# Attention with two gated layers on one core: run 0's q and k loaded, transposed and split by head pairs, and where the warm matmuls end

## The chip, the cores and the metric

The kernel runs on one core of a Trainium2 chip. The metric is device time in microseconds (us). Shares of the work fall to TensorE (PE, with PEld for its weight loads), VectorE (DVE), ScalarE (ACT), GpSimd (POOL) and the queue of SyncE (SP), from which all DMAs of this kernel are issued.

## What is computed

Windowed attention over 4 batches, 8 heads, 576 positions and head size 64 (each query sees itself and the 127 positions before it, with a bias by distance), then two gated layers over the 2304 tokens. Inputs are float32.

```python
def attention(q, k, v):                      # (4, 8, 576, 64)
    scores = 0.125 * q @ k.transpose(0, 1, 3, 2)
    rel = pos[:, None] - pos[None, :]
    scores = where((rel >= 0) & (rel < 128), scores - slope[h] * abs(rel), -1e9)
    p = exp(scores - scores.max(-1, keepdims=True))
    return (p / (p.sum(-1, keepdims=True) + 1e-9)) @ v

x = attention(q, k, v)                       # as (2304, 512)
x = ((x @ w_a) * (x @ w_b)) @ w_out          # 512 -> 1536 -> 512
out = (((x @ w1) * (x @ w2)) @ w3) @ w_out2  # 512 -> 1024 -> 1024 -> 512
```

## The kernel before

**Split numbers.** Every float32 product is made of three products of a high and a low part (`x_hi`, `x_lo`): ACT copies the high part, DVE subtracts it from the whole (`sub`, line 73). For q and k the parts are `q_th`, `q_tl`, `k_th`, `k_tl` (lines 291 and 292).

**Steps and runs.** A batch has five blocks of queries, four of 128 and one of 64. `RUNS` takes them as blocks (0, 1), (2, 3), (4). A step is one run for one pair of heads; with four pairs, steps 0 to 3 are run 0 of the first batch, steps 4 to 7 its run 1, steps 8 to 11 its run 2, and so on to 59. Step n issues (`attention_ops`, line 675): the scores of the step on PE (`scores`, line 318); on DVE four reductions with the bias, which also give the row's extreme (`step_exps`, line 345), and on ACT four exponentials with their sums (line 351); the product with v of step n - 3 (`pv`, line 404); then some gate work from `Filler`; and for step n - 1 the division on DVE (`norms`, lines 358 to 365: sum plus 1e-9, reciprocal, four multiplications) and the transposes of the quotients on PE (`probs`, line 383), which DVE or ACT copies out as `pt` (line 270 or 268).

**Loads and transposes of q and k.** `load_item` loads one block of q or of k for all 8 heads, 256 KB in pieces of 256 bytes. The first six (four of run 0, two of run 1) go to tiles named `early`, later ones to a ring of five named `raw`. `prep` transposes an item on PE (four transposes, line 282) and splits it. The four items of run 0 are loaded, transposed and split ahead of step 0; those of a later run during the run before it, one a step.

**Weights.** `Stages` (`side`) brings the six weight blocks of the first gate group through `convert`: load (lines 83, 92), two passes on ACT (lines 108, 111), four on DVE (lines 115, 118, 122, 127), the high part on ACT (line 136), the low part on DVE (line 73, tile `wlA`). For each step it makes `PACE` turns. Only two raw blocks are held at a time: a third is loaded when the first has been read.

**Gate work.** `Filler` holds the first group's gate matmuls (`g1`, line 546; `g2_some`, line 574) and gives some to PE in each step, from step 7 on, when the first 256 tokens have passed the attention.

**Warm matmuls.** `keep_warm` (line 373) issues matmuls on a tile of zeros whose result nobody reads: ten of 256 columns at the start, then one of 512 columns after each full block of `pv` of the first batch, two a step for the products of steps 0 to 7.

**What sets the order.** PE's instructions keep the order of the program (`manual_schedule`); those of the other engines are ordered by the scheduler at build time, which fixes each engine's queue. On the chip each engine then takes its queue in that order.

Of the kernel before, what the change touches and what calls it, by code (L numbers as in the profile page):

```python
# [8 lines left out]
F32 = mybir.dt.float32  # L9
# [20 lines left out]

GROUPS = (6, 4)
TA, TN = 256, 512
LEAD, EARLY, RING = 512, 6, 5
CUTS = (0, 1280, 1792, 2304)
RUNS = ((0, 1), (2, 3), (4,))
LAG = 3
# [1 line left out]
FILL = 1.6  # L38
PACE = (2.0, 1.0)
TURN = 400  # L40
WARM_RUNS, WARM = 3, 1


@with_exitstack
def attention_moe_moe(ctx, tc, q, k, v, w_a, w_b, w_o, w_1, w_2, w_3, w_o2, out):
# [193 lines left out]
    def items(run):  # L239
        return [(x, i) for i in blocks_of(run)[1] for x in range(2)] if run < NR else []  # L240
# [10 lines left out]

    def load_item(run, n):
        b, (x, i) = blocks_of(run)[0], items(run)[n]
        if len(items(0)) * run + n < EARLY:
            t = early_p.tile([P, H * D], F32, name="early")
        else:
            t = ring_p.tile([P, H * D], F32, name="raw")
        raws[b, x, i] = t
        load(t, x, b, i)

    def load_v(run, n):
        b, i = blocks_of(run)[0], blocks_of(run)[1][n]
# [9 lines left out]
    def prep(run, n):  # L272
        b, (x, i) = blocks_of(run)[0], items(run)[n]
        m = rows(i)
        hold = []

        def trans():
            ps = ps_t.tile([P, W], F32, name="tr")[:, 0:NP * m].rearrange("p (h c) -> p h c", h=NP)
            hold.append(ps)
            t = raws.pop((b, x, i))  # L280
            for hp in range(NP):
                nc.tensor.transpose(ps[:, hp, :], t[0:m, hp * P:(hp + 1) * P], ident[0:m, 0:m])  # L282

        def parted():
            ps = hold[0]
            if x == 0 and m == LAST:
                dst = [(slice(j * D, (j + 1) * D), q_t2, slice(j * D, (j + 1) * D)) for j in range(2)]
            else:
                dst = [(slice(0, P), k_t if x else q_t, slice(i * P, i * P + m))]
            for o, (hi, lo), c in dst:  # L290
                nc.scalar.activation(hi[o, :, c], ps[o], ACTF.Copy)
                sub(nc.vector, lo[o, :, c], ps[o], f32(hi[o, :, c]))

        return trans, parted

# [88 lines left out]
        t = d["pt"] = sm_p.tile([P, W], F32, name="pt", bufs=PTS)[:, 0:nj * n]  # L384
        evict(nc.scalar if i else nc.vector, t, ps)

    ready = [0]
    outs = {}

    def pv(step):  # L390
# [5 lines left out]
        for i in RUNS[rn]:  # L396
# [9 lines left out]
                        start=(g == 0), stop=(g == nb - 1),  # L406
                    )
            at += m
            if b == 0 and rn < WARM_RUNS and m == P:
                keep_warm(WARM, warm)  # L410

    def pv_out(step):
        b, rn, hp = step
# [261 lines left out]
    def attention_ops():  # L675

        late = []
        for n in range(NS + LAG):
# [5 lines left out]
            if n >= LAG:  # L684
                ops.append(lambda s=steps[n - LAG]: pv(s))
                late_1.append(lambda s=steps[n - LAG]: pv_out(s))
            if hp < len(items(run + 1)):
                f, h = prep(run + 1, hp)
                ops.append(f)
                late_1.append(h)  # L690
# [12 lines left out]
    class Filler:  # L703
# [5 lines left out]
        def run(self, owed):  # L709
            self.owed += owed  # L710
            while self.owed > 0 and self.items:
                f, cost, need = self.items[0]
                if whole.get(0, 0) < 6 or need > min(ready[0], CUTS[len(acc)]):
                    break
                self.items.pop(0)
                self.owed -= cost
                f()
            self.owed = min(self.owed, 1.0)

# [6 lines left out]
    pools["A", 1] = ctx.enter_context(tc.tile_pool(name="wA1", bufs=1))  # L726
    first = ExitStack()
    pools.update(conv=first.enter_context(tc.tile_pool(name="conv_a", bufs=1)), raws=2, cas=3)
    early_p = first.enter_context(tc.tile_pool(name="early_p", bufs=EARLY))
    pools["gate"] = gate_pa  # L730
    pools.update(abufs=1, gbufs=2)

    consts()
    for x in range(len(items(0))):
        load_item(0, x)
    for x in range(len(RUNS[0])):
        load_v(0, x)
    for x in range(len(items(1))):
        load_item(1, x)
        f, g = prep(0, x)  # L740
        f()
        g()
    side.parts += weight_parts(0)
    fl = Filler()
    nc.vector.memset(warm, 0.0)
# [66 lines left out]
```

## Time and profile before

| | |
|---|---|
| time, median of 3 runs | 963.18 us (962.84 to 963.54) |
| profiled execution | 965.76 us, span 964.0 us |
| PE busy | 944.0 us, 98% of the span |
| DVE busy | 552.1 us, 57% |
| ACT busy | 420.6 us, 44% |
| POOL busy | 156.9 us, 16% |
| share of PE in the chain that ended last | 91% |

Busy time is a mean over stages. The profiled execution is one execution: its rows give durations and waits, and its own time lies 2.58 us over the median. "Idle before" in a row is the time in which the engine had nothing to run, with the releaser that ended it. A row's duration reaches to the result; the next instruction of the engine may start somewhat before that.

### The profile page before, as it was taken

What the parts mean: (1) busy time and instruction counts of PE and PEld (TensorE: products, weight loads), DVE (VectorE), ACT (ScalarE), POOL (GpSimd) and SP (SyncE); (2) the same over time, 40 slices, a digit from 0 to 9 for tenths busy, and PEclk for the clock granted to TensorE, in tenths of its full rate; (3) what the DMA queues carried; (4) which work ended last, traced back from release to release, by engine and by line L of the source; (5) the groups of instructions that cost most, each with busy time, mean ns of one, the idle gap of its engine ahead of it and who ended that gap; (6) DMA issues with size and microseconds to landing.
All of it is one profiled execution on the core that took longest, in us unless ns stands there. A gap on an engine that the chain in (4) does not pass through costs nothing.

```text
span 964.0 us, 13974 instructions
## 1 busy us (share of the span) xinstructions
PE 944.0 (98%) x5330; PEld 787.4 (82%) x5330; DVE 552.1 (57%) x1312; ACT 420.6 (44%) x939; POOL 156.9 (16%) x139
## 2 busy tenths in 40 slices
PE   7899999999999999999999999999999999999998
PEld 5588788787888888888888888888888888888886
DVE  6968786854998355866745653822832822521322
ACT  5867777855654344444533531533421421211111
POOL 3000010001112110211110121344212111111111
PEclk8799999999999999999999999999999999999999
DMA  9523333002443222332312320300300300000112
GB/s 213 154 57 71 83 77 68 18 2 88 132 137 103 77 88 91 106 99 78 130 46 97 109 88 1 111 21 0 110 22 1 109 22 1 23 1 0 44 56 99
DMA packets 90371, 68.28 MB, mean 71 GB/s; under 512 B 58304, under 2 KB 79296, under 8 KB 90304
## 3 DMA queue, kind: packets, MB, share of 16 engines
q1 hardware_dynamic: 90304, 67.38, 24.1%
q8 instruction: 42, 0.69, 0.3%
q14 instruction: 25, 0.20, 0.1%
HBM read 58.20 MB, written 8.91 MB: 70 GB/s over the span
## 4 chain that ended last, share of the span: by engine, by line
PE 91%; DVE 5%; ACT 2%; DMA 1%; issue 0%; SPq 0%; POOL 0%; DVEq 0%
PE mm L546 51%; PE mm L598 13%; PE mm L613 10%; PE mm L454 5%; PE tr L404 3%; PE s L318 2%; PE tr L383 2%; PE mm L574 2%; PE tr L282 1%; DVE pe L345 1%; DVE pe L365 1%; ACT pe L351 1%; PE mm L446 1%; PE mm L586 1%; DMA early<-in_k 1%
## 5 line engine op out<-in xcount | busy, mean ns | idle before, releaser
L73 POOL TENSOR_TENSOR gl<-g,gh 128x512 fp32r<-128x512 f32 (+1 forms) x102 | 124.4, 1219 | 790.3 <-ACT gh L558 790.3
L555 DVE TENSOR_TENSOR g<-a,mm 128x512 f32<-128x512 f32 (+1 forms) x102 | 63.4, 622 | 203.1 <-PE mm L546 198.3
L558 ACT ACTIVATE gh<-g 128x512 fp32r<-128x512 f32 (+1 forms) x102 | 59.1, 579 | 152.9 <-DVE g L555 152.4
L553 ACT ACTIVATE a<-mm 128x512 f32<-128x512 f32 (+1 forms) x102 | 55.2, 541 | 126.2 <-PE mm L546 126.2
L546 PE MATMUL mm<-x_hi,wlA 128*128 128x512 f32 (+1 forms) x416 | 102.9, 368 | 0.0
L546 PE MATMUL mm<-x_lo,whA 128*128 128x512 f32 (+1 forms) x416 | 99.6, 361 | 0.0
L546 PE MATMUL mm<-x_hi,whA 128*128 128x512 f32 (+1 forms) x416 | 99.4, 361 | 0.0
L546 PE MATMUL mm<-x_hi,wlB 128*128 128x512 f32 (+1 forms) x400 | 98.9, 369 | 0.1
L546 PE MATMUL mm<-x_lo,whB 128*128 128x512 f32 (+1 forms) x400 | 98.6, 368 | 0.0
L546 PE MATMUL mm<-x_hi,whB 128*128 128x512 f32 (+1 forms) x400 | 98.2, 368 | 0.0
L111 ACT ACTIVATE ce<-raw,pad 128x512 int32<-128x512 uint32 x76 | 57.9, 762 | 65.9 <-DVE ca L127 33.8
L546 PEld LDWEIGHTS mm<-x_lo,whA 128*128 128x128 f32 x416 | 72.5, 189 | 12.2
L546 PEld LDWEIGHTS mm<-x_hi,whA 128*128 128x128 f32 x416 | 72.5, 189 | 12.0
L546 PEld LDWEIGHTS mm<-x_hi,wlB 128*128 128x128 f32 x400 | 71.1, 188 | 13.1 <-ACT acc L590 0.5
L546 PEld LDWEIGHTS mm<-x_lo,whB 128*128 128x128 f32 x400 | 71.1, 189 | 12.5
L546 PEld LDWEIGHTS mm<-x_hi,whB 128*128 128x128 f32 x400 | 71.0, 189 | 12.5
L602 DVE TENSOR_TENSOR acc<-acc,mm 128x512 f32<-128x512 f32 (+1 forms) x100 | 62.2, 629 | 33.1 <-PE mm L598 32.9
L546 PEld LDWEIGHTS mm<-x_hi,wlA 128*128 128x128 f32 x416 | 71.3, 189 | 11.6 <-issue 0.3
L108 ACT ACTIVATE ca<-raw 128x512 f32<-128x512 f32 x76 | 50.6, 666 | 51.0 <-DMA raw<-in_moe_w 23.2
L351 ACT ACTIVATE pe<-pe,st 128x256 f32<-128x256 f32 (+1 forms) x144 | 68.4, 478 | 9.7 <-DVE st L345 9.3
L127 DVE SCALAR_TENSOR_TENSOR ca<-ce,ca 128x512 int32<-128x512 int32 x76 | 58.9, 775 | 13.1 <-ACT ce L111 11.6
L122 DVE SCALAR_TENSOR_TENSOR ca<-raw,ca 128x512 int32<-128x512 int32 x76 | 58.8, 775 | 1.7
(121 smaller groups left out, 1579.2 us busy)
## 6 DMA issues: line engine op xcount, KB each, us to landing
raw<-in_moe_w SPq DMA_DIRECT2D x32, 512.0 KB, 3.6
raw<-in_moe_w_out SPq DMA_DIRECT2D x20, 512.0 KB, 3.5
raw<-in_moe_w_a SPq DMA_DIRECT2D x12, 512.0 KB, 3.6
raw<-in_moe_w_b SPq DMA_DIRECT2D x12, 512.0 KB, 3.5
out<-acc SPq DMA_DIRECT2D x18, 256.0 KB, 2.0
v<-in_v SPq DMA_DIRECT2D x16, 256.0 KB, 4.1
w<-ce SPq DMA_DIRECT2D x16, 256.0 KB, 2.0
raw<-w SPq DMA_DIRECT2D x16, 256.0 KB, 2.9
```

Of the source, the lines that this page charges most:

```text
L73: eng.tensor_tensor(out=out, in0=a, in1=b, op=ALU.subtract)
L111: nc.scalar.activation(e, lw, ACTF.Relu, bias=seven, scale=-(2.0 ** -29))
L122: nc.vector.scalar_tensor_tensor(out=ai, in0=hw, scalar=-(1 << 30), in1=ai, op0=ALU.bitwise_and, op1=ALU.bitwise_or)
L127: nc.vector.scalar_tensor_tensor(out=ai, in0=es[0], scalar=7, in1=ai, op0=ALU.bitwise_xor, op1=ALU.bitwise_or)
L351: nc.scalar.activation(pe[:, j, :n], pe[:, j, :n], ACTF.Exp, bias=st[:, 0, j:j + 1], scale=-1.0, accum_out=st[:, 1, j:j + 1],)
L546: nc.tensor.matmul(p, w[:, z, kk, :], x[:, kk, o], start=(y == 0), stop=(y == len(terms) - 1))
L553: nc.scalar.activation(a, ps[0], ACTF.Copy)
L555: nc.vector.tensor_tensor(out=gg, in0=a, in1=ps[1], op=ALU.mult)
L558: nc.scalar.activation(gh, gg, ACTF.Copy)
L598: nc.tensor.matmul(p, w, x, start=(y == 0), stop=(y == len(terms) - 1))
L602: nc.vector.tensor_tensor(out=ya, in0=ya, in1=p, op=ALU.add)
L613: nc.tensor.matmul(p, x, w, start=(y == 0), stop=(y == len(terms) - 1))
```

## The change

For run 0 of the first batch, `load_first` loads q and k by pairs of heads: for each pair and each of q and k two DMAs of 64 KB, one per block, in tiles `first`. The order of issue is pair 0 (q, then k), pair 1, the first v, pair 2, the second v, pair 3, then the four items of run 1. `prep_first` transposes a pair's q and k (four transposes) and splits each into parts of 256 columns. Pair 0 is prepared ahead of step 0; pair p + 1 is transposed and split within step p, behind the scores of that step. `EARLY` falls from 6 to 2 and then counts items of run 1. `keep_warm` inside `pv` is called until the filler has given out its first gate work (`began`), and no longer for all of the first batch's runs.

```diff
-LEAD, EARLY, RING = 512, 6, 5
+LEAD, EARLY, RING = 512, 2, 5
-WARM_RUNS, WARM = 3, 1
@@ load_item
-        if len(items(0)) * run + n < EARLY:
-            t = early_p.tile([P, H * D], F32, name="early")
+        if run == 1 and n < EARLY:
+            t = early_p.tile([P, H * D], F32, name=f"early{n}")
+    def load_first(hp, x):
+        t = raws[x, hp] = early_p.tile([P, 2, P], F32, name=f"first{x}{hp}")
+        for i in range(2):
+            nc.sync.dma_start(
+                out=t[:, i].rearrange("p (h d) -> p h d", h=2),
+                in_=(q, k)[x][0, 2 * hp:2 * hp + 2, i * P:(i + 1) * P, :].rearrange("h p d -> p h d"),
+            )
+    def prep_first(hp):
+        hold = []
+        def trans():
+            ps = ps_t.tile([P, W], F32, name="tr").rearrange("p (x i c) -> p x i c", x=2, i=2)
+            hold.append(ps)
+            for x in range(2):
+                raw = raws.pop((x, hp))
+                for i in range(2):
+                    nc.tensor.transpose(ps[:, x, i], raw[:, i], ident)
+        def parted():
+            for x, parts in enumerate((q_t, k_t)):
+                ps = hold[0][:, x].rearrange("p i c -> p (i c)")
+                hi, lo = [z[:, hp, 0:2 * P] for z in parts]
+                nc.scalar.activation(hi, ps, ACTF.Copy)
+                sub(nc.vector, lo, ps, f32(hi))
+        return trans, parted
@@ pv
-            if b == 0 and rn < WARM_RUNS and m == P:
-                keep_warm(WARM, warm)
+            if not began[0] and m == P:
+                keep_warm(1, warm)
@@ attention_ops
+            if run == 0 and hp + 1 < NP:
+                ops += prep_first(hp + 1)
@@ Filler.run
                 self.owed -= cost
+                began[0] = True
                 f()
@@ body
-    for x in range(len(items(0))):
-        load_item(0, x)
-    for x in range(len(RUNS[0])):
-        load_v(0, x)
+    for hp in range(NP):
+        for x in range(2):
+            load_first(hp, x)
+        if hp in (1, 2):
+            load_v(0, hp - 1)
     for x in range(len(items(1))):
         load_item(1, x)
-        f, g = prep(0, x)
+    for f in prep_first(0):
         f()
-        g()
```

The lines of the changed kernel are numbered otherwise: its 372 is line 345 of before, 385 to 392 are 358 to 365, 345 is 318, and 114, 117, 121, 126 are 115, 118, 122, 127.

**First place: the start of PE's queue.** In `tr` lie transposes, in `s` scores, `first` and `early` are loaded tiles. Before, from the last of the ten warm matmuls on:

```order
L373 MATMUL mm<-warm 128x256
L282 MATMUL tr<-ident,early 128x128 x16
L318 MATMUL s<-k_th,q_tl 128x128 x2
L318 MATMUL s<-k_tl,q_th 128x128 x2
L318 MATMUL s<-k_th,q_th 128x128 x2
L318 MATMUL s<-k_th,q_tl 128x256 x2
```

Now, from the last warm matmul on; two transposes of `first_143` stand ahead of the ten:

```order
L312 MATMUL tr<-ident,first_146 128x128 x2
L345 MATMUL s<-k_th,q_tl 128x128 x2
L345 MATMUL s<-k_tl,q_th 128x128 x2
L345 MATMUL s<-k_th,q_th 128x128 x2
L345 MATMUL s<-k_th,q_tl 128x256 x2
L345 MATMUL s<-k_tl,q_th 128x256 x2
L345 MATMUL s<-k_th,q_th 128x256 x2
L312 MATMUL tr<-ident,first_149 128x128 x2
L312 MATMUL tr<-ident,first_152 128x128 x2
L289 MATMUL tr<-ident,early_171 128x128 x4
```

Sixteen transposes ahead of the first scores have become four; the transposes of the first item of run 1 (`early_171`) stand between the scores of step 0 and those of step 1, as before.

**Second place: DVE's queue around the reductions of step 2.** `ca` is a weight block in conversion, `pe` and `st` are a step's exponents and sums. Before, from step 1's multiplications on (`st_274` is step 1, `st_348` step 2):

```order
L365 TENSOR_SCALAR pe_275<-pe_275,st_274 128x128 x2
L365 TENSOR_SCALAR pe_280<-pe_280,st_274 128x256 x2
L345 ISA pe_349,st_348<-s_334,relb_95 128x128
L345 ISA st_348 128x1
L345 ISA pe_354,st_348<-s_334,relb_95 128x256
```

Now (`st_280` is step 1, `st_363` step 2):

```order
L392 TENSOR_SCALAR pe_281<-pe_281,st_280 128x128 x2
L72 TENSOR_TENSOR k_tl_103<-tr_291,k_th_102 128x256
L392 TENSOR_SCALAR pe_286<-pe_286,st_280 128x256 x2
L114 TENSOR_SCALAR ca_251<-ca_251 128x512
L117 TENSOR_SCALAR ca_251<-ca_251 128x512
L372 ISA pe_364,st_363<-s_349,relb_95 128x128
L372 ISA st_363 128x1
```

The first two operations of the first weight block's conversion now stand ahead of step 2's reductions; before, they stood ahead of step 3's.

**Third place: DVE's queue around the multiplications of step 5.** Before (`st_567` is step 5, `st_644` step 6, `wlA1` a finished weight block):

```order
L359 RECIPROCAL st_567<-st_567 128x4
L115 TENSOR_SCALAR ca_396<-ca_396 128x512
L365 TENSOR_SCALAR pe_568<-pe_568,st_567 128x256 x2
L365 TENSOR_SCALAR pe_573<-pe_573,st_567 128x256 x2
L118 TENSOR_SCALAR ca_396<-ca_396 128x512
L358 TENSOR_SCALAR st_644<-st_644 128x4
L73 TENSOR_TENSOR wlA1_317<-ca_385,whA1_316 128x512
L122 SCALAR_TENSOR_TENSOR ca_396<-raw_330,ca_396 128x512
L359 RECIPROCAL st_644<-st_644 128x4
L115 TENSOR_SCALAR ca_465<-ca_465 128x512
L127 SCALAR_TENSOR_TENSOR ca_396<-ce_398,ca_396 128x512
```

Now (`st_591` is step 5, `st_668` step 6); the other three multiplications of step 5 follow behind the four reductions of step 6:

```order
L392 TENSOR_SCALAR pe_523<-pe_523,st_517 128x256
L72 TENSOR_TENSOR wlA1_332<-ca_489,whA1_331 128x512
L72 TENSOR_TENSOR x_lo_68<-tr_602,x_hi_67 128x256
L72 TENSOR_TENSOR k_tl_103<-tr_613,k_th_102 128x4x64
L385 TENSOR_SCALAR st_591<-st_591 128x4
L386 RECIPROCAL st_591<-st_591 128x4
L392 TENSOR_SCALAR pe_592<-pe_592,st_591 128x256
L372 ISA pe_669,st_668<-s_654,relb_95 128x256
```

Before, ten conversion operations follow step 5's multiplications in the queue (lines 118, 122 and 127 twice each, 115 once, three `wlA`); now none does, the `wlA1` shown is the last of the six blocks. PE's queue is otherwise the same up to the gate work, less six of the warm matmuls: those behind the products of steps 5, 6 and 7.

## Rows read from the trace of the kernel before

**Rows 1.** The page: busy time, share of the span and instructions of each engine.

```profile
PE 944.0 (98%) x5330; PEld 787.4 (82%) x5330; DVE 552.1 (57%) x1312; ACT 420.6 (44%) x939; POOL 156.9 (16%) x139
```

**Rows 2.** Waits of PE in 0 to 110 us: total us, times, longest.

```profile
PE tr L383 <- DVE pe L365: 7.0, 6, 2.2
```

**Rows 3.** Chain that ended last, 40 to 82 us: start us, us, what.

```profile
44.00 0.27 DVE pe L365
44.41 1.94 PE tr L383 x8
...
50.48 4.31 PE mm L546 x36
54.79 0.87 PE tr L383 x8
...
56.60 0.32 PE mm L373
...
66.68 0.32 PE mm L373
...
80.73 0.23 PE tr L383 x2
```

**Rows 4.** Busy time by stretch: length, PE, PEld, DVE, ACT, POOL, PEclk, DMA share, GB/s.

```profile
21.00:24.00 3.00, 3.00 (x24) 2.01 (x22) 2.79 (x12) 2.74 (x11) 0.00 (x0) 0.50 1.35 197
...
42.00:45.00 3.00, 0.79 (x4) 0.62 (x4) 3.00 (x11) 3.00 (x11) 0.00 (x0) 0.50 0.84 251
60.00:80.00 20.00, 20.00 (x195) 17.30 (x194) 11.79 (x49) 12.37 (x37) 1.46 (x2) 1.00 0.33 75
80.00:100.00 20.00, 18.24 (x179) 15.47 (x179) 18.06 (x78) 17.41 (x59) 0.73 (x1) 0.93 0.39 88
```

**Rows 5.** Instructions of PE in order, start of the kernel: start us, us, what, idle before.

```profile
2.83 2.31 PE L373 MATMUL mm<-warm 128*128 128x256 f16 x10 [2.83 <-DVE warm L745]
...
11.64 0.72 PE L282 MATMUL tr<-ident,early 128*128 128x128 f32 x4 [0.81 <-DMA early<-in_q]
12.29 0.47 PE L318 MATMUL s<-k_th,q_tl 64*128 64x128 f32 x2
```

**Rows 6.** Instructions of DVE in order, 9 to 52 us.

```profile
10.98 0.29 DVE L345 CUSTOM_DVE_ANT_0 pe<-s,relb 128x128 f32<-128x128 f32 x1 [0.71 <-PE s L318]
...
15.15 0.28 DVE L345 CUSTOM_DVE_ANT_0 pe<-s,relb 128x128 f32<-128x128 f32 x1
...
19.30 0.28 DVE L345 CUSTOM_DVE_ANT_0 pe<-s,relb 128x128 f32<-128x128 f32 x1
...
39.01 0.41 DVE L73 TENSOR_TENSOR k_tl<-tr,k_th 128x256 fp32r<-128x256 f32 x1
39.34 0.68 DVE L127 SCALAR_TENSOR_TENSOR ca<-ce,ca 128x512 int32<-128x512 int32 x1
39.94 0.68 DVE L122 SCALAR_TENSOR_TENSOR ca<-raw,ca 128x512 int32<-128x512 int32 x1
...
43.92 1.14 DVE L365 TENSOR_SCALAR pe<-pe,st 128x256 f32<-128x256 f32 x4
```

**Rows 7.** DMA issues of SP in order: start us, us the issue took.

```profile
0.72 0.44 SPq L247 DMA_DIRECT2D early<-in_q  x1
...
2.79 0.89 SPq L247 DMA_DIRECT2D early<-in_k  x1
...
6.41 1.14 SPq L247 DMA_DIRECT2D early<-in_q  x1
...
13.70 0.61 SPq L83 DMA_DIRECT2D raw<-in_moe_w_a  x1
```

**Rows 8.** DMA issues by line, 13.6 to 13.8 us: KB each, us to landing.

```profile
raw<-in_moe_w_a SPq DMA_DIRECT2D x1, 512.0 KB, 4.9
```

**Rows 9.** The same, issues near 2.8 and 6.4 us.

```profile
early<-in_k SPq DMA_DIRECT2D x1, 256.0 KB, 5.1
...
early<-in_q SPq DMA_DIRECT2D x1, 256.0 KB, 5.1
```

**Rows 10.** Instructions of ACT in order, first pass over the first weight block.

```profile
18.68 0.67 ACT L108 ACTIVATE ca<-raw 128x512 f32<-128x512 f32 x1
```

More of the change, by code (lines that the diff above doesn't have):

```diff
@@ L385, in probs @@
         evict(nc.scalar if i else nc.vector, t, ps)
-    ready = [0]
+    ready, began = [0], [False]
     outs = {}
@@ L728, in attention_moe_moe @@
     pools.update(conv=first.enter_context(tc.tile_pool(name="conv_a", bufs=1)), raws=2, cas=3)
-    early_p = first.enter_context(tc.tile_pool(name="early_p", bufs=EARLY))
+    early_p = first.enter_context(tc.tile_pool(name="early_p", bufs=1))
     pools["gate"] = gate_pa
```

## The prediction

> **What bounds the kernel now.** I read the page first: PE is busy 944.0 of 964.0 us [rows 1], so all its idle time together is 20 us, and only what moves PE counts. Then PE's waits: 7.0 us of them in the first 110 us are for DVE's multiplications of line 365 [rows 2]. Then the chain of waits [rows 3], where the reader is to see one hand-over: DVE holds the chain up to a row of line 365 at 44.00, which belongs to step 5; at 44.41 PE takes it with the transposes of step 5's quotients, begins the gate work at 50.48 and keeps the chain, in rows of PE alone, until 80.73. The table by stretch says why [rows 4]: DVE is busy 2.79 of 3 us in the first and 3.00 in the last of the eight stretches from 21 to 45 us (23.73 of 24 in all), while PE works 0.79 us in the last; from 60 to 80 us PE works 20.00 of 20 and DVE 11.79. So there are two regimes. Up to step 5's multiplications the end is set by DVE's queue; behind them by the number of PE's instructions. The stall at 80 to 100 us (PE 18.24 of 20) is fed by scores that PE itself issues, so it moves with PE and is no cushion.
>
> Two questions follow: when are step 5's multiplications done (now 43.92 + 1.14 = 45.06 [rows 6]), and what does PE do after that.
>
> **Warm matmuls.** Six go, those behind the products of steps 5 to 7. Their rows stand in PE's regime, from 56.60 to 66.68, 0.32 us each [rows 3]; nothing lies beside them. 6 x 0.32 = 1.9 us off the end. Those of steps 0 to 4 stay.
>
> **The start.** Before, four loads of 256 KB stand ahead of step 0; the fourth is issued at 2.79 and lands 5.1 us later, at 7.9 [rows 7, 9]. Pair 0 needs 256 KB in all; at 1.2 us for 256 KB (6.41 + 5.1 = 11.5, three loads and 3.6 us after 7.9) the saving is 3.6 us, and pair 0 is there at about 4.4. But PE's queue has pair 0's q transposes, then the ten warm matmuls, which took 2.31 us [rows 5], then the k transposes. So the k transposes run at about 6.3, copy and subtraction take 0.9, and the first reductions come at about 9, against 10.98 [rows 6]. That is a gain of 2 us (1 to 3) for step 0.
>
> It does not reach step 1. PE's queue has the transposes of run 1's first item ahead of step 1's scores, then as now; in the trace they waited for that load until 11.64, and the scores followed at 12.29 [rows 5]. The same 1.5 MB still stands ahead of it. So step 1's scores start where they did, and its reductions at about 14.4 against 15.15 [rows 6]: 0.7 earlier, because step 0's division is out of the way by then.
>
> **The conversions move forward.** This is the term that decides. The first two conversion operations now stand ahead of step 2's reductions. They need the first weight block, issued at 13.70 and landing 4.9 later, at 18.6 [rows 7, 8]. In the changed queue of SP the two loads of `relb2` (256 KB, 1.2 us) have come ahead of it, and sixteen issues stand where four did; I put its landing at 20.1. ACT's first pass takes 0.67 [rows 10], then the two operations 0.33 each, so step 2's reductions begin at about 21.5. Now they begin at 19.30 [rows 6]. That is 2.2 us later, of which DVE stands idle about 1.5. The bounds: if the block lands where it did, 18.6, DVE's own work ahead ends at about 19 and the reductions are 0.5 later; if every one of the sixteen issues takes the 0.44 us of the first [rows 7] instead of the 0.3 that its 64 KB need at the rate above, 16 x 0.14 = 2.2 us more, 4.4 later.
>
> From there on I count DVE's queue up to the end of step 5's multiplications, by how far each operation moves the next one: 0.33 for 256 columns and for lines 115 and 118, 0.60 for lines 122, 127 and `wlA` (39.01, 39.34, 39.94 [rows 6]). Before, the stretch took 45.06 - 19.30 = 25.8 us. The change puts into it:
>
> the ten conversion operations that stood behind step 5, 7 x 0.60 + 3 x 0.33 = +5.2; the first two now stand ahead of the stretch, -0.66; pair 3's two splits, 2 x 0.33 = +0.66; one `x_lo` of 256 columns falls behind the stretch, -0.33. Together +4.9 us.
>
> Nothing hides it: DVE has no gaps there. So step 5's multiplications end at about 21.5 + 25.8 + 4.9 = 52.2, 7.1 us after 45.06. Bounds of the second part: 4.0 if some reductions no longer wait for ACT and fit closer; 6.0 if DVE, with no conversion left to fill, waits twice for the scores of steps 6 and 7.
>
> **What PE makes of it.** From there PE has the same instructions to the gate work, 50.48 - 45.06 = 5.4 us, which began at a granted clock of 0.50, the lower of its two levels (1.2 and 2.4 GHz) [rows 4]; the gate begins at about 57.5. Behind it, conversions that overlapped with PE's own time are merely done already: PE waited for none of them, so that returns nothing. The extra instructions of the splits cost DVE 4 x 0.06 us, inside the count.
>
> **Sum.** +2.2 + 4.9 - 1.9 = +5.2 us. The profiled execution took 965.76, 2.58 over the median of 963.18; the difference is applied to the median: 963.2 + 5.2 = 968.4. With the low bounds, 0.5 + 4.0 - 1.9 = +2.6, 965.8; with the high ones, 4.4 + 6.0 - 1.9 = +8.5, 971.7.
>
> The smaller loads may also be weighed by a page. In the trace 256 KB pass in 1.2 us when loads of that size follow each other [rows 7, 9]. The Trainium skill, page "DMA: Bandwidth & Descriptors", section "Bandwidth", measures 138 GB/s for a single transfer of 64 KB and advises to batch to 1 MiB; no run here shows loads of 64 KB. By it, as an estimate, 1 MB in such pieces would take 7.6 us instead of 4.8 and all behind land 2.8 later.
>
> **Rivals.**
>
> *Faster: the early start carries through.* DVE's queue is fixed, but if the weight block landed before DVE asks for it, and the real limit in 12 to 27 us were PE at its lower clock rather than DVE, step 0's 2 us would reach the gate, and the conversions would run in gaps. For it: the granted clock is 0.50 in 21 to 24 us [rows 4]. Against: DVE is busy 3.00 of 3.00 us in most stretches from 24 us on, and ten operations more stand in its queue. It needs step 5 to end before 45.06, that is 7 us of DVE time found. It would give 963.2 - 2 - 1.9 = 959.3. Chance 12%.
>
> *Nearly no change.* Gate work begins some 2 us later and the warm matmuls pay for it: this needs most of the conversion work moved to be covered, for instance because DVE's waits for ACT in steps 2 to 5 vanish. 963.2 + 1.9 - 1.9 = 963.2. Chance 11%.
>
> *Slower still: the sixteen small loads hold back everything behind them.* The load of run 1's first item would land 2 to 3 us later, and with it step 1's scores, and the weight blocks after that. By the high end of the landing above, 968.4 + 2.2 = 970.6. For it: an issue takes 0.44 us even with nothing ahead [rows 7]. Against: the queue was full of bytes, not of issues, from 2.79 on (0.89, then 1.14 an issue). Chance 12%. By the estimate from the Trainium skill's page "DMA: Bandwidth & Descriptors" (section "Bandwidth") it would be 968.4 + 2.8 = 971.2.
>
> *Slower by the clock.* PE stands idle longer ahead of the gate work; if its first 36 matmuls (4.31 us) ran at the lower level, where eight transposes took 1.94 us against 0.87 later [rows 3], 4.3 us more: 972.7. Chance 3%.
>
> **Chances.** The forecast of about 968.4 has 62%. What a measurement of this kernel can tell from no change is about 0.2%, 1.9 us: under 961.3 is faster, over 965.1 slower. Slower: 62 + 12 + 3 less 4 for a forecast whose terms all come out low, 73%; same: 11 + 3 = 14%; faster: 12 + 1 = 13%. A range from 962.5 to 971.8 holds the forecast, the third case and the even one, and leaves out the faster one and the clock.
>
> **What would show it.** In the profile of the changed kernel: the first reductions (line 372) at about 9; step 1's scores at 12 to 13, behind a wait of PE for the load of run 1's first item; a wait of DVE or ACT for the first weight block at about 20 and step 2's reductions at 21.5; the last of the six `wlA` ahead of step 5's multiplications; these ending at about 52 and the first matmul of line 573 (546 before) at about 57; no warm matmul after that and PE in one piece to about 86. I am wrong if step 5's multiplications end before 47: then either the block landed in time or DVE had room that its rows don't show.

## The result, and the profile after

| | before | changed |
|---|---|---|
| time, median of 5 runs each | 963.27 us (962.84 to 965.75) | 972.26 us (972.10 to 974.23) |
| ratio, 95% interval | | 1.0095 (1.0081 to 1.0109) |
| profiled execution | 965.76 us, span 964.0 us | 974.23 us, span 972.4 us |

Slower, as forecast, but by 9.0 us instead of 5.2; 972.26 lies above the range (962.5 to 971.8). The spans differ by 8.4 us. PE has the same matmuls less six and nearly the same busy time [rows 1], so the loss is idle time of PE. The page of the changed kernel:

```profile
PE 943.8 (97%) x5324; PEld 788.7 (81%) x5324; DVE 555.8 (57%) x1316; ACT 421.0 (43%) x943; POOL 156.4 (16%) x139
```

Waits of PE in the first 120 us (total us, times, longest). Where before had 7.0 us for DVE's multiplications [rows 2], now the largest are for a split of q and k, high part on ACT (line 318) and low part on DVE (`k_tl`, line 72; 2.0 of its 3.7 us are one wait of step 5's scores for run 1's k, not for a pair):

```profile
PE s L345 <- ACT k_th L318: 5.7, 3, 3.8
PE tr L410 <- DVE pe L392: 3.9, 3, 1.5
PE s L345 <- DVE k_tl L72: 3.7, 3, 2.0
PE tr L289 <- DMA early<-in_q: 2.8, 1, 2.8
```

The same from 120 us on. The two middle rows are new:

```profile
PE tr L410 <- DVE pe L392: 1.9, 2, 1.5
PE mm L481 <- DVE w3l L475: 1.2, 1, 1.2
PE mm L473 <- DVE ca L126: 0.8, 1, 0.8
PE mm L601 <- POOL gl L72: 0.4, 1, 0.4
```

DMA issues of SP (start, us the issue took; compare [rows 7]). Two issues of 64 KB take 0.95 us; run 1's first item, issued at 6.41 before, is issued at 10.13; the first weight block at 17.00 instead of 13.70:

```profile
0.72 0.95 SPq L263 DMA_DIRECT2D first<-in_q  x2
...
10.13 0.47 SPq L246 DMA_DIRECT2D early<-in_q  x1
...
17.00 0.62 SPq L82 DMA_DIRECT2D raw<-in_moe_w_a  x1
```

PE in order (start, us, what, idle before and who ended it; compare [rows 5]). Step 1's scores start at 14.56 behind that item, and step 3's wait twice, for the high part (3.77) and for the low one (0.87):

```profile
13.51 1.11 PE L289 MATMUL tr<-ident,early 128*128 128x128 f32 x4 [2.85 <-DMA early<-in_q]
14.56 0.47 PE L345 MATMUL s<-k_th,q_tl 64*128 64x128 f32 x2
...
28.24 0.48 PE L345 MATMUL s<-k_th,q_tl 64*128 64x128 f32 x2 [3.77 <-ACT k_th L318]
29.59 0.47 PE L345 MATMUL s<-k_tl,q_th 64*128 64x128 f32 x2 [0.87 <-DVE k_tl L72]
```

ACT between the reductions of step 2 and these scores. Pair 3's two copies (line 318) stand behind the exponentials of step 2 (line 378) and behind passes over the weights (110, 135):

```profile
24.17 0.39 ACT L378 ACTIVATE pe<-pe,st 128x128 f32<-128x128 f32 x1
...
25.04 0.36 ACT L318 ACTIVATE q_th<-tr 128x256 fp32r<-128x256 f32 x1
...
26.66 0.74 ACT L110 ACTIVATE ce<-raw,pad 128x512 int32<-128x512 uint32 x1
27.30 0.61 ACT L135 ACTIVATE whA<-ca 128x512 fp32r<-128x512 f32 x1
27.82 0.36 ACT L318 ACTIVATE k_th<-tr 128x256 fp32r<-128x256 f32 x1
```

DVE (compare [rows 6]): the first reductions of steps 0 to 3, the wait for the first weight block, and the end of step 5's multiplications, 54.83 + 0.87 = 55.70:

```profile
9.78 0.29 DVE L372 CUSTOM_DVE_ANT_0 pe<-s,relb 128x128 f32<-128x128 f32 x1 [1.65 <-PE s L345]
...
16.35 0.29 DVE L372 CUSTOM_DVE_ANT_0 pe<-s,relb 128x128 f32<-128x128 f32 x1 [0.37 <-PE s L345]
...
22.73 0.43 DVE L114 TENSOR_SCALAR ca<-ca 128x512 f32<-128x512 f32 x1 [1.46 <-ACT ca L107]
...
23.53 0.28 DVE L372 CUSTOM_DVE_ANT_0 pe<-s,relb 128x128 f32<-128x128 f32 x1
...
31.90 0.29 DVE L372 CUSTOM_DVE_ANT_0 pe<-s,relb 128x128 f32<-128x128 f32 x1
...
54.83 0.87 DVE L392 TENSOR_SCALAR pe<-pe,st 128x256 f32<-128x256 f32 x3
```

The chain that ended last (compare [rows 3]): gate work from 58.93, PE alone to 87.24, where before had 50.48 and 80.73:

```profile
58.93 4.31 PE mm L573 x36
...
87.24 0.23 PE tr L410 x2
```

The span's 8.4 us are thus 8.45 to the start of the gate work, less 1.93 for the warm matmuls (80.73 to 87.24 is 6.51), plus the 2.0 us of the two new late waits (at 346 and 514 us).

### The profile page after: what moved, and what is told of

Its sections match the earlier page's. It is cut to its first block, busy times and chain, and to the rows that moved or that the text cites. A ratio compares the mean times of both kernels' runs of the same rounds, so it can differ in the third digit from the quotient of the medians.

```text
span 972.4 us, 13970 instructions
## 1 busy us (share of the span) xinstructions
PE 943.8 (97%) x5324; PEld 788.7 (81%) x5324; DVE 555.8 (57%) x1316; ACT 421.0 (43%) x943; POOL 156.4 (16%) x139
## 4 chain that ended last, share of the span: by engine, by line
PE 91%; DVE 4%; ACT 2%; SPq 2%; DMA 1%; issue 0%; POOL 0%; DVEq 0%; ACTq 0%
PE mm L573 51%; PE mm L625 12%; PE mm L640 10%; PE mm L481 5%; PE tr L431 3%; PE s L345 3%; PE tr L410 3%; PE mm L601 2%; PE tr L289 1%; DVE pe L372 1%; ACT pe L378 1%; DVE pe L392 1%; SPq L263 1%; SPq L246 1%; PE mm L473 1%; PE mm L613 1%
## 5 line engine op out<-in xcount | busy, mean ns | idle before, releaser
L121 DVE SCALAR_TENSOR_TENSOR ca<-raw,ca 128x512 int32<-128x512 int32 x76 | 62.0, 817 | 1.6
```

What stands on the lines that cost most here:

```text
L121: nc.vector.scalar_tensor_tensor(out=ai, in0=hw, scalar=-(1 << 30), in1=ai, op0=ALU.bitwise_and, op1=ALU.bitwise_or)
```

## The experiments

Each time stands beside runs of the kernel before on the same chip (medians 963.1 to 963.6); "ratio" is to these, with its 95% interval.

### One part of the change at a time

**Warm matmuls alone**: `before` with the part of the change that ends the warm matmuls (`began`), nothing else.

> The kernel before with only the last part of the change: the six warm matmuls behind the products of steps 5 to 7 are gone; loads and order are those of before. My account of the change: 1.9 us less, 963.2 - 1.9 = 961.3, step 5's multiplications still end near 45 us and the gate work begins near 50.5. In the changed kernel 2.0 us were lost late, in two waits of PE for DVE (0.8 us near 310 to 400 us, 1.2 us near 510 to 600 us). If these waits come from the earlier end of the warm matmuls, they appear here too and the time is 963.2; if they come from the loads and the order of the start, they are absent here. A rival in which the warm matmuls kept the clock up would give 964 or more, with a granted clock under 1.00 in the first 10 us of the gate work.

Measured 963.51 us, ratio 0.9994 (0.9983 to 1.0005): nothing gained. The late waits are there, with loads and order at the start as before (waits of PE from 120 us on):

```profile
PE tr L382 <- DVE pe L364: 2.0, 2, 1.5
PE mm L453 <- DVE w3l L447: 1.2, 1, 1.2
PE mm L445 <- DVE ca L126: 0.8, 1, 0.8
```

**Loads and splits alone**: the changed kernel, warm matmuls as before.

```diff
-            if not began[0] and m == P:
+            if b == 0 and m == P:
                 keep_warm(1, warm)
```

> The changed kernel with the warm matmuls of the first batch kept as before; loads, transposes and splits as changed. My account: step 5's multiplications end near 55.7 us and the gate work begins near 58.9, as in the changed kernel, and six warm matmuls more at 0.32 us: 972.3 + 1.9 = 974.2, if the two late waits of PE (0.8 and 1.2 us) stay. If the late waits belong to the end of the warm matmuls, they are gone here and the time is 972.2. If the loads were harmless and the end of the warm matmuls were the cost, the time would be near 963.

Measured 971.67 us, ratio 1.0085 (1.0071 to 1.0099), without the two late waits. So the waits belong to the warm matmuls' end, and the loss to the start.

**The counter.** Every matmul tile, a warm one too, advances `turn` in `mm_tile`, which picks the PSUM pool; behind the attention there are four, and six turns fewer shift all later tiles by two. One line undoes that:

```diff
+    turn[0] += 6
     fixed.close()
     ring.close()
```

With it, PE's instructions behind the attention stand in the order of before again. In the kernel before without the six warm matmuls:

> The kernel before without the six warm matmuls behind the products of steps 5 to 7, as in the run of that part alone, but the counter that picks the PSUM pool of each matmul tile (turn, in mm_tile) is advanced by six where the attention ends, so that every later tile lies where it lay before. Theory: the two late waits of PE (0.8 and 1.2 us, in the products of w3) come from that counter: each warm matmul took one turn, six fewer shift the four pools by two, and the order behind the attention changes. Then both waits are gone, the whole 1.9 us of the six matmuls is kept, and the time is 963.4 - 1.9 = 961.5. Rival (the warm matmuls' end itself costs 2 us later, by the clock or otherwise): 963.4 as in the run of the part alone.

Measured 961.21 us, ratio 0.9979 (0.9969 to 0.9989). The two waits are gone (same view as above); this kernel beats both:

```profile
PE tr L382 <- DVE pe L364: 2.0, 2, 1.5
PE mm L573 <- POOL gl L72: 0.4, 1, 0.4
```

The same line in the changed kernel:

> The changed kernel as it is, but the counter of the matmul tiles is advanced by six where the attention ends. If the two late waits of PE (0.8 and 1.2 us) come from the counter here too, they are gone and the time is 972.3 - 2.0 = 970.3; if they come from the loads or the order at the start, it stays at 972.3.

Measured 968.93 us, ratio 1.0052 (1.0038 to 1.0066), and no late waits: 3.3 us less, where the two waits are 2.0. The rest is within the two intervals together, and the granted clock of the profiled changed kernel was 0.91 in 100 to 120 us against 1.00 here; no run separates the two.

### Loads undone, splits left in the steps

**Half of the small loads issued from ACT's queue.**

```diff
-            nc.sync.dma_start(
+            (nc.sync, nc.scalar)[x].dma_start(
                 out=t[:, i].rearrange("p (h d) -> p h d", h=2),
```

> The changed kernel, but the eight small loads of k are issued from ACT's queue instead of SP's. Theory 1 (SP's queue is bound by the number of its issues, 0.51 us from one to the next, not by bytes): the first item of run 1 is issued 8 x 0.51 = 4.1 us earlier, near 6.0 instead of 10.13, step 1's scores begin near 12 instead of 14.56, the first weight block is issued near 13 and lands near 18 instead of 22.0; as DVE's queue holds all thirty conversion operations ahead of step 5's multiplications here as well, the end of these moves with the block, from 55.7 to about 52, the gate work from 58.9 to about 55, and the time is about 968.5. Rival (the transfers of 64 KB themselves are slow, or bytes bind): issue of the item earlier, but its landing stays near 13, the weight block near 22, and the time stays at 972.

**Four loads of 256 KB**, as before; pairs transposed and split within the steps.

```diff
-            load_first(hp, x)
...
+        raws[0, x, i] = early_p.tile([P, H * D], F32, name=f"whole{n}")
+        load(raws[0, x, i], x, 0, i)
...
-                    nc.tensor.transpose(ps[:, x, i], raw[:, i], ident)
+                    nc.tensor.transpose(ps[:, x, i], raw[i][:, hp * P:(hp + 1) * P], ident)
```

> The changed kernel, but run 0's q and k come in the four loads of 256 KB of before; transposes and splits by pairs within the steps stay, and so does the end of the warm matmuls. Theory 1 (number of issues): run 1's first item is issued near 6.4 and lands near 11.5, step 1's scores begin near 12.3, the first weight block lands near 18.6, step 5's multiplications end 3.4 us earlier than in the changed kernel, near 52.3, and the time is about 969. What then stays over 961.3 (before less six warm matmuls) is the price of the order in DVE's queue alone, 5 to 7 us. Rival (all of the loss comes from the small loads, the order is harmless): about 961 to 963.

Measured 975.76 us (1.0127, 1.0110 to 1.0144) and 976.71 us (1.0132, 1.0113 to 1.0151): both slower than the changed kernel, against every forecast. Run 1's first item was issued earlier (7.72 in the first), but step 1's reductions did not come earlier (16.65 and 17.79), and the build answered the earlier weights by moving seven and nine conversion operations, instead of two, ahead of step 2's reductions. Theory 1 in this form fell: the loads are not what step 1 and step 2 wait for here. Two things were mixed, and the next runs hold one of them fixed.

### Is it the order of DVE's queue?

DVE's queue is held to a given order of reductions, multiplications and conversion operations by edges of order between neighbours (`keys` is the list, `marks` the recorded instructions, the third argument is shortened here; lines of these kernels are shifted by some 17). DVE's splits and copies and the queues of the other engines stay with the build:

```diff
+    for x, y in zip(keys, keys[1:]):
+        tc.add_manual_dep(marks[y], marks[x].name, NoSync, reason="order")
```

The changed kernel in the order of before:

> The changed kernel, with its loads, transposes and splits by pairs and its warm matmuls, but DVE's queue is held to the order of before for the reductions, the multiplications and the thirty conversion operations up to step 7 (edges of order only, no waits). Theory (the order of the conversions in DVE's queue makes the loss): step 2's reductions follow step 1's multiplications at about 21.3 instead of 23.53 us, from there to the end of step 5's multiplications 25.8 + 0.7 for pair 3's splits, 47.8 instead of 55.7, gate work from about 52 instead of 58.6, time 972.3 - 6.5 = about 965.8. What is then left over 963.4 are the late start of step 1 and the two late waits of PE, less the warm matmuls. Rival (the sixteen small loads or the work by pairs make the loss, whatever the order): 970 to 972.

Measured 972.71 us, ratio 1.0100 (1.0085 to 1.0115): nothing gained. DVE (idle before in brackets): with the conversions out of the way, step 2's reductions come at 21.95, but DVE then stands idle for pair 3's copy on ACT, and again for the scores; step 3's reductions come at 29.87:

```profile
21.95 0.29 DVE L389 CUSTOM_DVE_ANT_0 pe<-s,relb 128x128 f32<-128x128 f32 x1 [0.52 <-PE s L362]
...
26.24 0.42 DVE L80 TENSOR_TENSOR q_tl<-tr,q_th 128x256 fp32r<-128x256 f32 x1 [2.18 <-ACT q_th L335]
...
29.87 0.29 DVE L389 CUSTOM_DVE_ANT_0 pe<-s,relb 128x128 f32<-128x128 f32 x1 [1.63 <-PE s L362]
```

The mirror, the kernel before in the order of the changed one:

> The mirror of it: the kernel before, with its loads, its transposes and all its warm matmuls, but DVE's queue is held to the order that the changed kernel has for reductions, multiplications and conversion operations up to the first multiplications of step 5. Theory (order of the conversions): step 2's reductions wait for the first weight block, 20.0 instead of 19.3 us, ten more conversion operations lie ahead of step 5's multiplications, which end at 45.06 + 0.7 + 5 = 51 to 52 us; the gate work begins at 55 to 56 and the time is 963.4 + 5 = about 968.5 (967.5 to 970). Rival (the order is harmless, the loads make the loss): 963 to 964.

Measured 971.82 us, ratio 1.0083 (1.0068 to 1.0099). The order alone costs the kernel before 8 us, more than I had counted; the gate work begins at 56.55 (50.48 in before), near the forecast of 55 to 56. Its scores then wait for DVE's reductions (waits of PE, 8 to 66 us):

```profile
PE s L334 <- DVE st L361: 7.6, 7, 2.2
```

Together: either the order or something else in the changed start is enough for the loss, and undoing the order alone changes nothing. In the changed kernel the conversions moved forward into gaps that the steps leave.

**Fewer conversions ahead of step 5** than before, in the kernel of 961.21 us (the list of before, seven operations moved):

> The kernel of the first of these runs (before without the six warm matmuls, counter kept), with seven conversion operations more behind step 5's multiplications than before: 13 ahead of them instead of 20. If the end of step 5's multiplications is set by what lies ahead of them in DVE's queue, they end at 45.1 - 7 x 0.5 = about 41.6 us (not before step 5's exponentials, about 41), the gate work begins about 3 us earlier, and the time is 961.5 - 3 = 958.5. If the later steps or the gate's weights then come too late, PE waits for them behind the first gate work and the time stays at 961.5.

Measured 961.55 us, ratio 0.9976 (0.9966 to 0.9986): no gain over 0.9979, although step 5's multiplications ended at 41.40 and the gate work began at 44.29, 4.3 us earlier than in that kernel (48.56). PE's order: the gate work soon waits for a weight (line 564) and for step 6's multiplications:

```profile
44.29 0.82 PE L564 MATMUL mm<-x_hi,wlA 128*128 128x256 f32 x4
...
49.06 0.71 PE L564 MATMUL mm<-x_hi,wlA 128*128 128x256 f32 x4 [1.56 <-DVE wlA L80]
...
51.65 1.23 PE L401 MATMUL tr<-ident,pe 128*128 128x128 f32 x8 [0.92 <-DVE pe L382]
```

So the start of the gate work is no measure of the end by itself: here what DVE had put off, a weight and step 6's multiplications, stopped PE behind it.

### Loads and place of the split, taken apart

All of these have the counter kept and no warm matmuls behind step 4's products. Those called "held" have the reductions, multiplications and conversions of DVE's queue in the order of before. Against 961.21 us not only the loads and the place of the split differ: that kernel splits by blocks, in parts of 512 columns, and all of these by pairs of heads, in parts of 256. 256 KB with all pairs split ahead of step 0, which would separate the form of the split from the loads, was not run. The place changes by such lines (here two steps ahead):

```diff
-            if run == 0 and hp + 1 < NP:
-                ops += prep_first(hp + 1)
+            if run == 0 and hp + 2 < NP:
+                ops += prep_first(hp + 2)
...
-    for f in prep_first(0):
-        f()
+    for hp in range(2):
+        for f in prep_first(hp):
+            f()
```

Small loads, all pairs split ahead of step 0, order left to the build, and held:

> The sixteen small loads in the changed kernel's order, but all four pairs are transposed and split ahead of step 0, as before; no warm matmuls behind step 4's products, counter kept, so that it differs from the kernel of 961.2 us (before without six warm matmuls, counter kept) in the loads alone. DVE's queue has 18 conversion operations ahead of step 5's multiplications, 20 in that kernel. Theory (splitting within the steps made the loss, the small loads cost only their issue time): pair 3 lands near 11, step 0's reductions begin near 13 instead of 10.4, the weights come 3.4 us later; 1 to 3.5 us more, 962 to 964.7. Rival (the small loads make the loss): 968 to 970.

> The first of these runs with DVE's queue held to the order of before. It shows what the small loads cost by themselves when nothing else differs from the kernel of 961.2 us: the late start of step 0 (about 2.5 us) and the later weights (3.4 us), of which the conversions have some to spare. 962.5 to 964.5; as fast as 961.2 if all of it is hidden, 966 or more if DVE's fixed queue waits for the weights.

Small loads, split two steps ahead, order left to the build, and held:

> The changed kernel, but pairs 0 and 1 are transposed and split ahead of step 0 and pair p + 2 within step p, so that the scores of a step no longer wait for a split of the step just before; counter kept. The build puts 28 conversion operations ahead of step 5's multiplications, nearly as many as in the changed kernel (30). Theory A (chain through the steps: scores wait for a split that is queued behind the step's exponentials and behind conversions): steps 1 to 3 begin their reductions some 4 us apart as before instead of 6.6 to 8.4, PE's waits for k_th and k_tl (9.7 us in the changed kernel) fall under 2, and the time falls to 962 to 966. Theory B (the number of conversion operations ahead of step 5 decides): little change, 968 to 971.

> The same, and DVE's queue held to the order of before for reductions, multiplications and conversions (20 ahead of step 5's multiplications). If the chain and the order are two causes, each enough for the loss, this cures both: step 5's multiplications end at 46 to 48 us and the time is 961 to 965. If it stays at 968 or more, a third cause is at work.

The last of these with k's loads on ACT's queue:

> The kernel of 966.6 us (small loads, pairs split two steps ahead, order of before, counter kept), but the eight small loads of k are issued from ACT's queue. Theory (the loss that is left comes from SP's issue time): run 1's first item is issued at 7.7 instead of 10.1 and the first weight block near 15.2 instead of 17.1, step 1's reductions begin near 14.5 instead of 16.5, time 963 to 965. Rival (bytes or the size of the transfers): item and block land as late as now, 966 to 967.

Loads of 256 KB, split one step ahead and two steps ahead, held:

> Four loads of 256 KB as before, pairs 1 to 3 transposed and split within the step ahead of theirs as in the changed kernel, DVE's queue held to the order of before, no warm matmuls behind step 4's products, counter kept: it differs from the kernel of 961.2 us in the place of the splitting alone. Theory (chain through the steps): scores of steps 1 to 3 wait for k_th and k_tl, the reductions of steps 1 to 3 come 6 us or more apart, time 965 to 969. Rival (the splitting within steps costs nothing where the loads are early and the order is that of before): 961 to 962.5.

> The first of these runs, but pairs 0 and 1 are split ahead of step 0 and pair p + 2 within step p. If the distance of one step was the cause, the waits of PE for k_th and k_tl are gone and the time is 960.5 to 962.5, that of the kernel of 961.2 us; if any work by pairs within the steps costs, 964 or more.

Small loads, split one step ahead (the changed kernel), held:

> The changed kernel with the counter advanced and DVE's queue held to the order of before up to step 7: small loads and splitting one step ahead together, nothing else different from the kernel of 961.2 us. From the run without the counter (972.7, two late waits in it): 970.7. Had the two causes added up, 961.2 + 5.5 + 10.3 = 977; the small loads bring pair 0 earlier, so I expect the lower value, 970 to 971.5.

| us (ratio, 95% interval) | split ahead of step 0 | two steps ahead | one step ahead |
|---|---|---|---|
| loads of 256 KB, held | 961.21 (0.9979, .9969 to .9989), split by blocks; order of before not held but the same | 965.82 (1.0023, 1.0014 to 1.0032) | 971.48 (1.0083, 1.0069 to 1.0097) |
| small loads, held | 966.68 (1.0030, 1.0019 to 1.0041) | 966.62 (1.0025, 1.0014 to 1.0036) | 970.32 (1.0064, 1.0051 to 1.0077) |
| small loads, k on ACT's queue, held | | 964.43 (1.0009, .9999 to 1.0018) | |
| small loads, order of the build | 966.37 (1.0026, 1.0010 to 1.0042) | 968.47 (1.0047, 1.0033 to 1.0061) | 968.93 (1.0052, 1.0038 to 1.0066) |

Two of these lie inside their forecasts: small loads one step ahead, and k on ACT's queue. With all pairs split ahead, both times lie above the theory; in the held one DVE waits 1.15 us for the first weight block, the case of 966 or more that its text names. Two steps ahead, the held small loads (966.62) lie between their two forecasts and the 256 KB (965.82) in the second; 256 KB one step ahead (971.48) lies above its theory.

What follows. *The place of the split*, along a row: one step ahead instead of two costs about 6 us with loads of 256 KB (1.0083 against 1.0023) and about 4 with small loads (1.0064 against 1.0025). *The size of the loads*, down a column: two steps ahead it makes no difference (1.0025 against 1.0023), and one step ahead the small loads are, if anything, the faster (1.0064 against 1.0083). They bring pair 0 sooner (step 0's reductions at 9.2 instead of 11.6 us) and the first weight block later (issued at 17.01 instead of 13.39). *The first column is no such pair*: the 5 us between 961.21 and the small loads (0.9979 against 1.0030) are loads and form of split together, and against the two columns with like splits I can't put them down to the loads. Small loads and one step ahead together came to 8 us over 961.21 (1.0064), not to the sum of 977 that the last text works out.

The 4 us between 961.21 and 256 KB split two steps ahead are place and form together, against my forecast. The trace says where they lie, not why: step 0's reductions begin 1.03 us later (11.45 and 10.42), and from there to the end of step 5's multiplications DVE works 1.62 us longer and stands idle 1.85 us longer (columns as [rows 4]; first 961.21, then this kernel):

```profile
10.42:44.28 33.86, 25.53 (x187) 18.02 (x188) 31.91 (x128) 28.62 (x87) 0.00 (x0) 0.84 0.93 204
```

```profile
11.45:48.78 37.33, 28.85 (x196) 19.12 (x196) 33.53 (x130) 28.71 (x87) 0.00 (x0) 0.80 0.81 177
```

With the order left to the build and the split two steps ahead (27 conversions ahead of step 5's multiplications in its trace), theory A had the waits right, 0.9 us for k_th and k_tl instead of 9.7, but the time, 968.47, was in theory B's range: its steps come some 5 us apart (16.52, 21.36, 26.75). Left to the build, two steps instead of one gained only 0.5 us (968.47 against 968.93, within the intervals); holding the order then gave 2 us. So there the order does count, as in the kernel before; where the split is one step ahead it counts for nothing. With all pairs split ahead the build itself puts 20 ahead, as before, so that holding could change little (966.37 and 966.68).

What late issues cost, as far as one run shows it: with half of the issues elsewhere run 1's first item left at 8.85 instead of 10.14 and the first weight block at 16.16 instead of 17.09, step 1's reductions began at 15.16 instead of 16.47, and 1.5 us came back (1.0009 against 1.0025; the intervals overlap a little, so this is likely and no more). Issues of SP in that kernel:

```profile
8.85 0.47 SPq L263 DMA_DIRECT2D early<-in_q  x1
...
16.16 0.63 SPq L94 DMA_DIRECT2D raw<-in_moe_w_a  x1
```

and in its twin with all issues on SP:

```profile
10.14 0.47 SPq L263 DMA_DIRECT2D early<-in_q  x1
...
17.09 0.62 SPq L94 DMA_DIRECT2D raw<-in_moe_w_a  x1
```

The chain of the steps in the kernel with loads of 256 KB and the split one step ahead (PE, start of the scores of steps 1, 2 and 3, idle before):

```profile
14.82 0.47 PE L362 MATMUL s<-k_th,q_tl 64*128 64x128 f32 x2 [1.52 <-ACT k_th L335]
16.46 0.47 PE L362 MATMUL s<-k_tl,q_th 64*128 64x128 f32 x2 [1.17 <-DVE k_tl L80]
...
23.57 0.47 PE L362 MATMUL s<-k_th,q_tl 64*128 64x128 f32 x2 [2.49 <-ACT k_th L335]
...
29.01 0.33 PE L362 MATMUL s<-k_th,q_tl 64*128 64x128 f32 x2 [0.23 <-ACT k_th L335]
```

Reductions of steps 0 to 3 begin there at 11.55, 18.04, 25.75 and 30.79; in the kernel of 961.21 us at 10.42, 14.59, 18.74 and 21.58.

## Why the prediction was right and wrong

**Direction: right. Size: 5.2 us forecast, 9.0 measured.** In the profiles, over the forecast of 5.2: +2.0 from the first weight block (point 4), +1.5 from DVE's queue (point 5), -2.2 from PE (point 6) and +2.0 from two late waits that it had put at nothing (point 1) make 8.5, where the spans differ by 8.4. By its own steps, as points:

1. *Six warm matmuls, -1.9.* Right in size (0.9979 with the counter kept, 2.0 us), but "nothing lies beside them" overlooked that each of them also takes a turn in the choice of pool. The changed order behind the attention gave the 2.0 us back in two waits, at 346 and 514 us. No step of the prediction looked there.
2. *Step 0's reductions at about 9.* 9.78.
3. *Step 1's scores "start where they did", because "the same 1.5 MB still stands ahead" of run 1's first item.* Wrong: 14.56 instead of 12.29. Not the bytes counted but the issues, 0.51 us from one to the next; the item was issued 3.7 us later, though it landed 3.3 us after its issue instead of 5.1. The high bound had priced sixteen issues at 0.44 each and had that right, but only for the weights. The Trainium skill's page "DMA: Bandwidth & Descriptors", section "Bandwidth", read as an estimate in the prediction, gave 2.8 us for everything behind; the page's table was measured with DMAs issued from GpSimd, here SP issues them. The item landed 13.4 - 11.5 = 1.9 us later, 0.9 less than that estimate, and not for want of rate: here the engines had room (stretch from 6 to 12 us below: DMA share 0.85, before 1.34).
4. *Step 2's reductions at 21.5, +2.2 with a high bound of +4.4.* 23.53, +4.2. The first weight block was issued at 17.00 and landed 5.0 later; 1.46 us of DVE's idle time there, as forecast (1.5).
5. *DVE's queue to the end of step 5's multiplications, +4.9.* 55.70 - 23.53 = 32.2 instead of 25.8: +6.4, a little over the high bound. As a count it held: DVE works 30.51 us in that stretch and 25.48 in before (lines below), +5.0; the rest is idle time, 1.43 us of it one wait for step 5's exponentials (1.66 in all, 0.28 in before). As a cause it did not: with these operations put back behind step 5 the time stayed at 972.7, where the count gives 965.8. The step that failed is that DVE's queue alone sets the pace up to there. I took the pair splits as 0.33 us of DVE each and said that DVE has no gaps. The runs show that the split of a pair is a link in a chain: transposes, copy on ACT behind the exponentials of the step, subtraction on DVE, and only then the scores of the next step. The steps then come 6.6, 7.2 and 8.4 us apart (9.78, 16.35, 23.53, 31.90) instead of 4.2, 4.2 and 2.8; the first of these distances comes from the late load of run 1's first item (point 3), the others hold the chain, the second also 1.46 us of waiting for the weight block. The conversions stood in the gaps; with them put back behind step 5, DVE idled instead (2.18 and 1.63 us ahead of step 3's reductions). That the order alone can cost as much in the kernel before is a second fact. Each is enough for the loss, and that the count came near is in this sense luck.
6. *5.4 us from there to the gate work.* 2.9 to 3.2: the granted clock was 1.00 from 55.70 to 58.93, against 0.58 from 45.06 to 50.48 in before, and two of the eight transposes were already done.

Granted clock and DMA share, columns as [rows 4], of the changed kernel and then of before:

```profile
6.00:12.00 6.00, 3.32 (x18) 2.15 (x16) 2.27 (x11) 2.66 (x10) 3.19 (x4) 1.00 0.85 192
```

```profile
6.00:12.00 6.00, 4.56 (x27) 3.16 (x27) 3.78 (x11) 3.07 (x7) 3.20 (x4) 1.00 1.34 218
```

The same columns for point 5: from step 2's reductions to the end of step 5's multiplications, in the changed kernel and then in before (DVE is the third busy time), and DVE's longest wait in it:

```profile
23.53:55.70 32.17, 23.52 (x147) 15.24 (x145) 30.51 (x107) 25.24 (x71) 0.00 (x0) 0.65 0.56 131
```

```profile
19.30:45.06 25.76, 20.94 (x144) 13.14 (x144) 25.48 (x98) 22.27 (x66) 0.00 (x0) 0.77 0.78 181
```

```profile
52.77 0.17 DVE L385 TENSOR_SCALAR st<-st 128x4 f32<-128x4 f32 x1 [1.43 <-ACT pe L378]
```

**The rivals.** *The sixteen small loads hold back everything*, which I had given 12%, was right about the start: run 1's first item landed 1.9 us later, step 1's scores began 2.3 later and the first weight block landed 3.4 later, and its 970.6 is nearer than the forecast. But with like splits loads of 256 KB are no faster (971.48 against 970.32), so that the loss does not hang on these loads; half of the issues taken elsewhere gave 1.5 us. *Nearly no change* and *faster* had nothing behind them. *Slower by the clock* did not show: the first 36 gate matmuls took 4.31 us as before.

**The 9 us in parts**, by the ratios, 1% being 9.63 us: six warm matmuls -2.0 (0.9979), the loads and the split one step ahead together +7.0 (1.0052 against 0.9979), the counter +4.1 (1.0095 against 1.0052), of which 2.0 us are seen as waits. Each part is uncertain by 2 us or so, which may be all that the rest of the last one is. Open stay the 4 to 5 us that the held kernels cost over 961.21 even where no pair is split one step ahead (3 with k on ACT's queue): form of the split, its place and the loads are not separated there.

## What to carry to other kernels

Work moved from a prologue into the steps of a pipeline is priced by the chain it joins, not by its busy time: write down who needs its result and behind what it is queued on each engine. Two steps ahead instead of one was worth 6 and 4 us here with DVE's order held, and next to nothing with the order left to the build. When a build reorders a queue, an order that looks like the cause may only fill gaps; hold the order fixed in one run and transplant it into the other kernel in a second. And look for state that a removed instruction also advanced, such as a buffer counter: one line kept the whole gain of the warm matmuls.

## What was not expected of the hardware

An issue of a 64 KB DMA on SP took 0.44 to 0.58 us (median 0.47) and the next began 0.04 us later, where the first issue of 256 KB took 0.44 [rows 7]: sixteen of them and two of v kept the queue busy for 9.4 us, until 10.13. A 64 KB load landed 2.0 to 3.3 us after its issue (median 2.2) and one of 256 KB behind such loads after 3.3 us, against 5.1 in a full queue [rows 9]. DMA issues of the changed kernel (KB each, median us to landing), near 1 us and near 10.1 us:

```profile
first<-in_q SPq DMA_DIRECT2D x2, 64.0 KB, 2.0
...
early<-in_q SPq DMA_DIRECT2D x1, 256.0 KB, 3.3
```
